# First loads of an attention + MoE kernel: k halves on two hardware queues, q halves by GpSimd, one staging buffer for the global queries and keys

## The chip, the cores and the metric

The kernel runs on one core of one Trainium2 chip. The core has five engines that run at their own pace and meet through semaphores: PE (TensorE, matrix products into the accumulator memory PSUM), DVE (VectorE), ACT (ScalarE), POOL (GpSimd) and SP (SyncE, which only issues transfers here). Transfers between the chip's memory and the core's SBUF run on 16 DMA engines that all issuers share; SP, ACT and POOL each have a queue of their own. Only POOL's transfers change the type on the way (f32 in memory to bf16 in SBUF).

The metric is the device time of one execution in microseconds (us). Beside it stands the profile of one execution: its span is the time between the first and the last instruction, a little less than the execution's own time.

## The reference

```
k_all = concat(k_g, k_l); v_all = concat(v_g, v_l)          # B=8, H=8, Sg=32, Sl=512, D=64
out_g = softmax(scale * q_g @ k_all.T) @ v_all              # 32 global queries see everything
s_ll  = where(|i-j| <= 32, scale * q_l @ k_l.T, -1e9)       # local queries see a band ...
s_lg  = scale * q_l @ k_g.T                                 # ... and the 32 global keys
out_l = softmax(concat(s_lg, s_ll)) @ concat(v_g, v_l)
x     = concat(out_g, out_l) as (8*544 tokens, 512)
h     = x @ w_in                                            # 512 -> 2048
out   = (h * sigmoid(1.702 h)) @ w_out                      # 2048 -> 512, f32
```

## The kernel before

Work is done batch by batch. A batch has two quads of four heads (`Quad(0)` and `Quad(1)` are the two of batch 0, named `a` and `c` in the code; `Wide` quads are all later ones). A quad's attention feeds `xL[b]`, the batch's hidden rows; `h_mm`/`h_step` multiply them by `w_in` and apply the activation (tanh form), `o_mm` multiplies by `w_out`. After the first batch, attention of the next batch is woven between these products, and PE is busy nearly without a break. The order on every engine is the order in which the code is written (a manual schedule); each engine runs its own instructions strictly in that order.

The change lies in the first 10 us, in how batch 0's first quad is fed. A quad needs its queries and keys as bf16 with the head dimension on the partitions. Data come in row layout into `rk` (keys) and `rq` (queries), and DVE transposes them: `Tk` into `kT`, `Tq` into `qt`, here in two halves each, (0,8) and (8,16). The 32 global queries and keys of the quad go the same way: `load_g32` brings them in f32, `cast_g32` (DVE) writes bf16 into `rqg`/`rkg`, `transpose_g` (DVE) gives `qgT`/`kgT`. `ext` then copies global queries from `qgT` into free rows beside the local queries (`qt`), for four windows c = 0 to 3 of keys, so that one product serves both.

How the first quad's inputs come in, in the kernel before:

- ACT's queue issues both k halves in f32 (line 144); ACT casts them to `rk` (line 651).
- SP's queue issues the global queries (line 132), then q's second half in f32 (line 146; ACT casts it, line 658), then the global keys (line 132).
- POOL's queue issues q's first half, cast on the way (line 145), then the mask's step function (line 153), then quad 1's k and q (line 81), the global values, v, constants, and the weights `w_in` (line 256; the first product `h_mm` waits for the third of these eight transfers).

Then the order on PE is: seven warm-up products (line 179), the additive band masks of quad 0 (`a.B`, line 337), filler products on zeros (`zero`, line 648), scores `a.S(0)` in two parts, `a.S(1)` and right behind it, in the same function, the global-by-global scores `gk` (line 373, global keys x global queries; they need `kgT`), more fillers, `c.B(0)`, `a.K()` (global keys x all local queries), `c.S(0)`, and so on up to `h_mm` (line 588). ACT runs the exponentials `X(0)` (line 387) and `X(1)` (line 382, four pieces; piece 2 holds the `gk` scores), then `XK`.

`qt` has 24 rows of 32; its first and last four are cleared by eight DVE memsets (lines 184, 185). `S` reads of these rows only the columns that `ext` writes.

Of the kernel before, what the change touches and what calls it, by code (L numbers as in the profile page):

```python
# [12 lines left out]
F32 = mybir.dt.float32  # L13
BF16 = mybir.dt.bfloat16
FP8 = mybir.dt.float8e4
AF = mybir.ActivationFunctionType
# [4 lines left out]
def kernel(  # L21
# [12 lines left out]
    nc = tc.nc  # L34

    B, H, Sl, D = q_l.shape
# [20 lines left out]
    consts = ctx.enter_context(tc.tile_pool(name="consts", bufs=1))  # L57
# [8 lines left out]
    qf = q_l.rearrange("b (u j) (r t) d -> b (j r) u (t d)", j=4, t=16)  # L66
    kf = k_l.rearrange("b (u j) (r t) d -> b (j r) u (t d)", j=4, t=16)
    qgf = q_g.rearrange("b (u j) s d -> (j s) (b u) d", j=4)
    kgf = k_g.rearrange("b (u j) s d -> (j s) (b u) d", j=4)
# [4 lines left out]
    def load(b, us=(0, 1), names="qk"):  # L74
        if b not in loaded:
            loaded[b] = (ld.tile([128, 2, 16 * D], BF16, name="rk"),
                         ld.tile([128, 2, 16 * D], BF16, name="rq"))
        s = slice(us[0], us[-1] + 1)
        for name in names:
            dst, src = ((loaded[b][0], kf), (loaded[b][1], qf))[name == "q"]  # L80
            nc.gpsimd.dma_start(out=dst[:, s], in_=src[b][:, s])  # L81
# [34 lines left out]
    def load_turned(eng, out_, in_):  # L116
        eng.dma_start(out=out_[32:128], in_=in_[0:96])  # L117
        eng.dma_start(out=out_[0:32], in_=in_[96:128])  # L118
# [5 lines left out]

    g32 = {}

    def load_g32(name, src):
        t = g32[name] = consts.tile([128, 2, D], F32, name="g32%s" % name)
        if name == "v":
            load_turned(nc.sync, t, src[:, 0:2, :])  # L130
        else:
            nc.sync.dma_start(out=t, in_=src[:, 0:2, :])

    def cast_g32(name, t):
        nc.vector.tensor_copy(t[:, 0:2, :D], g32[name])

    load(0, names="")
    rk, rq = loaded[0]
    early = ld.tile([128, 4, TB], F32, name="early", bufs=1)
    k32 = early[:, 0:2].rearrange("p a b -> p (a b)")  # L140
    halves = (slice(0, 8 * D), slice(8 * D, 16 * D))
    load_g32("q", qgf)
    for f in halves:
        nc.scalar.dma_start(out=k32[:, f], in_=kf[0][:, 0, f])
    nc.gpsimd.dma_start(out=rq[:, 0, halves[0]], in_=qf[0][:, 0, halves[0]])  # L145
    nc.sync.dma_start(out=early[:, 2], in_=qf[0][:, 0, halves[1]])
    load_g32("k", kgf)

    warm = consts.tile([128, 512], BF16)
    nc.vector.memset(warm, 0.0)  # L150
# [3 lines left out]
        out=step, in_=step, pattern=[[1, 289]], compare_op=ALU.is_ge,  # L154
# [26 lines left out]
    qtiles = []  # L181
    for i in range(4):
        qt = consts.tile([128, 24, 32], F32, name="q%d" % i)
        nc.vector.memset(qt[:, 0:4, :], 0.0)
        nc.vector.memset(qt[:, 20:24, :], 0.0)
        qtiles.append(qt)

    qgT = consts.tile([128, NQ, 40], F32)
# [44 lines left out]
    def transpose_g(lo, hi, names="qk"):  # L233
        for name, dst, s in (("q", qgT, rqg), ("k", kgT, rkg)):
            if name not in names:
                continue
            nc.vector.transpose(dst[:, lo:hi, :32], s[:, lo:hi].bitcast(F32))
# [406 lines left out]
    a, c = Quad(0), Quad(1)  # L644
# [2 lines left out]
        for _ in range(n):  # L647
            nc.tensor.matmul(ps[:m, :w], lhsT=warm[:, :m], rhs=warm[:, :w], start=False, stop=False, skip_group_check=True)

    def cast_k(f):  # L650
        nc.scalar.activation(rk[:, 0, f], k32[:, f], AF.Copy)

    cast_k(halves[0])
    cast_k(halves[1])
    cast_g32("q", rqg)
    transpose_g(0, 2, "q")
    a.ext((0, 1), True)
    nc.scalar.activation(rq[:, 0, halves[1]], early[:, 2], AF.Copy)
    a.Tk(0, 8)
    a.Tk(8, 16)  # L660
    a.Tq(0, 8)
    a.Tq(8, 16)
    a.ext((2, 3))
    cast_g32("k", rkg)
    transpose_g(0, 2, "k")
    load_rest()
# [9 lines left out]
    zero(16, a.bk[1][3], 32, 32)  # L676
    a.X(1)
    c.Tk()
    c.ext((0, 1))
    c.Tq()  # L680
    c.ext((2, 3))
    c.B(0)
    a.K()
    a.XK()
# [59 lines left out]
    a, c = nq[1]  # L744
# [41 lines left out]
    a, c = nq[2]  # L786
# [122 lines left out]
```

## Time and profile before

| | us |
|---|---|
| time, median of 3 executions | 299.23 (299.15 to 299.37) |
| the profiled execution's own time | 299.14 |
| its span | 297.4 |
| PE busy | 289.9 (97%) |
| DVE / ACT / POOL busy | 218.7 / 165.5 / 81.9 |
| DMA engines | 90% or more busy from 7.4 to 44.6 us, 70% in the first 7.4 us |

How to read it: the span is cut by the program's order into a front, some 18 us in which batch 0's attention is built up and PE is often waiting or running fillers, and the rest, in which PE goes from product to product. A row of the timeline gives the start, the busy time, the engine and line, the operation with its output and inputs, how many instructions were merged into the row, and in square brackets how long the engine had been idle and what ended that. A row of the transfers gives the median time from the start of the issuing instruction to the landing of the data. The share of DMA is the summed time of packets on 16 engines, and can exceed 1 since packets overlap on an engine.

### The profile page before, as it was taken

What the parts mean: (1) busy time and instruction counts of PE and PEld (TensorE: products, weight loads), DVE (VectorE), ACT (ScalarE), POOL (GpSimd) and SP (SyncE); (2) the same over time, 40 slices, a digit from 0 to 9 for tenths busy, and PEclk for the clock granted to TensorE, in tenths of its full rate; (3) what the DMA queues carried; (4) which work ended last, traced back from release to release, by engine and by line L of the source; (5) the groups of instructions that cost most, each with busy time, mean ns of one, the idle gap of its engine ahead of it and who ended that gap; (6) DMA issues with size and microseconds to landing.
All of it is one profiled execution on the core that took longest, in us unless ns stands there. A gap on an engine that the chain in (4) does not pass through costs nothing.

```text
span 297.4 us, 8162 instructions
## 1 busy us (share of the span) xinstructions
PE 289.9 (97%) x3403; PEld 149.8 (50%) x3444; DVE 218.7 (74%) x440; ACT 165.5 (56%) x252; POOL 81.9 (28%) x133
## 2 busy tenths in 40 slices
PE   8999999999999999999999999999999999999995
PEld 4544446445454455445454455445544455445653
DVE  6679888979867887778877887788878866683320
ACT  4827465585556745576447654666546651663421
POOL 8884630589565002700072003500000000000000
PEclk9999999999999999999999999999999999999999
DMA  7999994596999613961299115901130022101122
GB/s 177 178 206 211 204 160 86 119 138 100 192 212 160 124 37 68 150 122 29 47 96 178 29 41 87 109 0 39 36 72 2 2 48 63 35 2 35 35 66 78
DMA packets 59316, 28.06 MB, mean 94 GB/s; under 512 B 47376, under 2 KB 49808, under 8 KB 59280
## 3 DMA queue, kind: packets, MB, share of 16 engines
q0 software_dynamic: 51728, 17.70, 53.1%
q1 hardware_dynamic: 7264, 9.31, 12.3%
q8 instruction: 27, 0.44, 0.6%
q10 hardware_dynamic: 288, 0.52, 0.5%
q14 instruction: 9, 0.07, 0.1%
HBM read 36.31 MB, written 8.91 MB: 152 GB/s over the span
## 4 chain that ended last, share of the span: by engine, by line
PE 92%; POOL 3%; DMA 3%; issue 1%; ACT 0%; POOLq 0%
PE op L613 39%; PE hp L588 38%; PE s L533 6%; PE ov L559 5%; DMA w_in_sb<-in_moe_w_in_dram 3%; PE s L588 1%; PE op L625 1%; POOL v L243 1%; PE og L570 1%; POOL w_in_sb L256 0%; PE s L559 0%; POOL rq L145 0%; POOL rvg L117 0%; PE og L458 0%; POOL rvg L118 0%
## 5 line engine op out<-in xcount | busy, mean ns | idle before, releaser
L613 PE MATMUL op<-w_out_sb,gT 128*128 128x512 bf16 x497 | 119.4, 379 | 1.8 <-issue 0.3
L596 DVE SCALAR_TENSOR_TENSOR gT<-th,hp 128x512 bf16<-128x512 f32 (+1 forms) x140 | 91.0, 656 | 39.7 <-ACT th L595 38.7
L588 PE MATMUL hp<-xL,w_in_sb 128*128 128x512 bf16 x488 | 108.4, 379 | 0.4
L595 ACT ACTIVATE th<-hp 128x512 f32<-128x512 f32 (+1 forms) x140 | 79.8, 573 | 43.0 <-PE hp L588 41.1
L588 PEld LDWEIGHTS <-w_in_sb 128*128 128x128 bf16 x576 | 56.1, 98 | 64.2 <-issue 0.5
L613 PEld LDWEIGHTS <-gT 128*128 128x128 bf16 x528 | 49.3, 98 | 54.9
L544 ACT ACTIVATE e<-s 128x1016 bf16<-128x1016 f32 (+1 forms) x56 | 53.3, 1005 | 7.4 <-PE s L533 7.1
L628 ACT ACTIVATE ob<-op 128x512 f32<-128x512 f32 x32 | 18.9, 599 | 62.3 <-PE op L613 62.3
L97 POOL DMA_DIRECT2D v<-in_v_l_dram x35 | 28.1, 806 | 82.1 <-PE og L570 74.0
L549 DVE TENSOR_TENSOR e<-e,mask 128x1712 bf16<-128x1712 bf16 (+1 forms) x27 | 28.4, 1051 | 3.4 <-ACT e L544 3.4
L464 DVE STREAM_TRANSPOSE sT<-ov 128x512 f32<-128x512 f32 x15 | 10.7, 716 | 14.4 <-PE ov L559 12.6
L473 DVE TENSOR_TENSOR xL<-ov,rs 128x512 bf16<-128x512 f32 x30 | 19.4, 686 | 1.9 <-PE ov L440 0.5
L533 PE MATMUL s<-q,kT 32*128 32x160 bf16 (+3 forms) x672 | 19.2, 243 | 0.0
L533 PEld LDWEIGHTS <-kT 32*128 32x128 bf16 x672 | 13.1, 94 | 12.0 <-issue 6.9
L507 DVE STREAM_TRANSPOSE kT<-rk 128x512 f32<-128x512 f32 x14 | 14.5, 1035 | 0.7 <-DMA rk<-in_k_l_dram 0.7
L99 POOL DMA_DIRECT2D v<-in_v_g_dram x24 | 14.1, 586 | 0.6 <-issue 0.5
L468 DVE STREAM_TRANSPOSE rs<-rT 128x512 f32<-128x512 f32 x16 | 11.4, 711 | 0.6
L559 PE MATMUL ov<-e,v 128*32 128x128 bf16 (+3 forms) x624 | 11.7, 223 | 0.0
L312 DVE STREAM_TRANSPOSE q<-rq 128x512 f32<-128x512 f32 (+1 forms) x17 | 11.4, 672 | 0.1
L559 PEld LDWEIGHTS <-v 128*32 128x32 bf16 x672 | 10.5, 97 | 0.0
L588 PE MATMUL hp<-xG,w_in_sb 128*128 128x256 bf16 x64 | 9.6, 273 | 0.1
L81 POOL DMA_DIRECT2D rk<-in_k_l_dram x10 | 6.4, 639 | 2.6 <-DMA w_out_sb<-in_moe_w_out_dram 2.0
(103 smaller groups left out, 158.8 us busy)
## 6 DMA issues: line engine op xcount, KB each, us to landing
out_dram<-ob SPq DMA_DIRECT2D x128, 64.0 KB, 1.8
v<-in_v_l_dram POOLq DMA_DIRECT2D x28, 96.0 KB, 4.8
rq<-in_q_l_dram POOLq DMA_DIRECT2D x5, 512.0 KB, 6.5
rk<-in_k_l_dram POOLq DMA_DIRECT2D x5, 512.0 KB, 8.5
w_in_sb<-in_moe_w_in_dram POOLq DMA_DIRECT2D x8, 256.0 KB, 8.6
w_out_sb<-in_moe_w_out_dram POOLq DMA_DIRECT2D x4, 512.0 KB, 11.1
v<-in_v_l_dram POOLq DMA_DIRECT2D x11, 128.0 KB, 6.4
rk<-in_k_l_dram POOLq DMA_DIRECT2D x5, 256.0 KB, 9.1
```

The costliest lines, as they stand in the source:

```text
L97: nc.gpsimd.dma_start(out=vt[0:n, :, c, :D], in_=vs[FIRST[c] : FIRST[c] + n])
L473: nc.vector.tensor_mul(self.x[:, 2 * self.u + h, :], self.st[1 + h], self.st["rs"])
L507: nc.vector.transpose(flat[:, 0:Sl].rearrange("p (r t) -> p t r", t=16), loaded[self.b][0][:, self.u].bitcast(F32))
L533: nc.tensor.matmul(bank(self.ps, j)[:, at : at + n], lhsT=self.k[p, KEYS[c] : KEYS[c] + 128, e], rhs=self.q[p, lo:hi, r0 : r0 + nr, e], st ...
L544: nc.scalar.activation(self.E[rnd][:, 2 * i : 2 * i + 2, :n], self.ps[i][:, :, :n], AF.Exp, scale=scale)
L549: eng.tensor_mul(e, e, mask[:, rnd : rnd + 1, :n].to_broadcast([128, 4, n]))
L559: nc.tensor.matmul(ov[32 * j : 32 * j + 32, :].rearrange("p (t r) -> p t r", t=16)[:, t0:t1, r0 : r0 + nr], lhsT=lv, rhs=self.E[rnd][:, j, ...
L588: nc.tensor.matmul(hp[:, : width(i)], lhsT=w_in_c[:, fc // 8, kc, fc % 8 // 2, :, fc % 2], rhs=(xL[i] if i < B else xG)[:, kc, :], start=( ...
L595: nc.scalar.activation(th[:, :n], hp[:, :n], AF.Tanh, scale=0.851)
L596: nc.vector.scalar_tensor_tensor(gTs[i][:, fc, :n], in0=th[:, :n], scalar=1.0, in1=hp[:, :n], op0=ALU.add, op1=ALU.mult)
L613: nc.tensor.matmul(op, lhsT=gTs[i][:, fc, tci * 128 : tci * 128 + 128], rhs=w_out_sb[:, fc, :], start=(first and fc == 4 * f4), stop=(fc = ...
L628: nc.scalar.activation(ob, op, AF.Copy, scale=0.5)
```

## The change

- The two k halves are issued first, one on ACT's queue and one on SP's queue, instead of both on ACT's.
- The global queries follow k's second half on SP's queue. Before, they were first there.
- Both q halves come through POOL's casting transfers, one behind the other. q's second half no longer goes through SP in f32, and ACT's cast of it is gone.
- Global queries and keys share one f32 buffer `stage`. So the transfer of the global keys is issued by SP only when DVE's cast of the global queries has read the buffer. Before, they had buffers of their own and both transfers were issued at the start.
- DVE's order begins with `a.Tk(0, 8)`, then the cast and transpose of the global queries, then `a.Tk(8, 16)`, `a.Tq` twice, then the cast and transpose of the global keys, then `c.Tk` and `c.Tq`.
- All four `ext` copies of quad 0 and all four of quad 1 run on ACT, before `X(0)`. Before, two ran on ACT and six on DVE.
- The eight memsets of `qt` are gone.

```diff
+    stage = consts.tile([128, 2, D], F32, name="stage")
+
     def load_g32(name, src):
-        t = g32[name] = consts.tile([128, 2, D], F32, name="g32%s" % name)
-        if name == "v":
-            load_turned(nc.sync, t, src[:, 0:2, :])
-        else:
-            nc.sync.dma_start(out=t, in_=src[:, 0:2, :])
+        g32[name] = stage
+        nc.sync.dma_start(out=stage, in_=src[:, 0:2, :])
 ...
+    for f, eng in zip(halves, (nc.scalar, nc.sync)):
+        eng.dma_start(out=k32[:, f], in_=kf[0][:, 0, f])
     load_g32("q", qgf)
     for f in halves:
-        nc.scalar.dma_start(out=k32[:, f], in_=kf[0][:, 0, f])
-    nc.gpsimd.dma_start(out=rq[:, 0, halves[0]], in_=qf[0][:, 0, halves[0]])
-    nc.sync.dma_start(out=early[:, 2], in_=qf[0][:, 0, halves[1]])
-    load_g32("k", kgf)
+        nc.gpsimd.dma_start(out=rq[:, 0, f], in_=qf[0][:, 0, f])
 ...
-        nc.vector.memset(qt[:, 0:4, :], 0.0)
-        nc.vector.memset(qt[:, 20:24, :], 0.0)
 ...
-    cast_k(halves[0])
-    cast_k(halves[1])
+    for f in halves:
+        nc.scalar.activation(rk[:, 0, f], k32[:, f], AF.Copy)
+    a.Tk(0, 8)
     cast_g32("q", rqg)
+    load_g32("k", kgf)
     transpose_g(0, 2, "q")
-    a.ext((0, 1), True)
-    nc.scalar.activation(rq[:, 0, halves[1]], early[:, 2], AF.Copy)
-    a.Tk(0, 8)
+    a.ext(act=True)
+    c.ext(act=True)
     a.Tk(8, 16)
     a.Tq(0, 8)
     a.Tq(8, 16)
-    a.ext((2, 3))
     cast_g32("k", rkg)
     transpose_g(0, 2, "k")
 ...
     c.Tk()
-    c.ext((0, 1))
     c.Tq()
-    c.ext((2, 3))
     c.B(0)
```

More of the change, by code (lines that the diff above doesn't have):

```diff
@@ L138 @@
     rk, rq = loaded[0]
+    halves = (slice(0, 8 * D), slice(8 * D, 16 * D))
     early = ld.tile([128, 4, TB], F32, name="early", bufs=1)
     k32 = early[:, 0:2].rearrange("p a b -> p (a b)")
-    halves = (slice(0, 8 * D), slice(8 * D, 16 * D))
+    for f, eng in zip(halves, (nc.scalar, nc.sync)):
+        eng.dma_start(out=k32[:, f], in_=kf[0][:, 0, f])
     load_g32("q", qgf)
     for f in halves:
-        nc.scalar.dma_start(out=k32[:, f], in_=kf[0][:, 0, f])
-    nc.gpsimd.dma_start(out=rq[:, 0, halves[0]], in_=qf[0][:, 0, halves[0]])
-    nc.sync.dma_start(out=early[:, 2], in_=qf[0][:, 0, halves[1]])
-    load_g32("k", kgf)
+        nc.gpsimd.dma_start(out=rq[:, 0, f], in_=qf[0][:, 0, f])
     warm = consts.tile([128, 512], BF16)
@@ L648, in zero @@
             nc.tensor.matmul(ps[:m, :w], lhsT=warm[:, :m], rhs=warm[:, :w], start=False, stop=False, skip_group_check=True)
-    def cast_k(f):
+    for f in halves:
         nc.scalar.activation(rk[:, 0, f], k32[:, f], AF.Copy)
-    cast_k(halves[0])
-    cast_k(halves[1])
+    a.Tk(0, 8)
     cast_g32("q", rqg)
+    load_g32("k", kgf)
     transpose_g(0, 2, "q")
-    a.ext((0, 1), True)
-    nc.scalar.activation(rq[:, 0, halves[1]], early[:, 2], AF.Copy)
-    a.Tk(0, 8)
+    a.ext(act=True)
+    c.ext(act=True)
     a.Tk(8, 16)
```

## The prediction

> **What bounds the kernel now.** I read the chain of waits first, to see where a shift in the first 10 us would end.
>
> ```profile
> 10.59 7.73 DMA w_in_sb<-in_moe_w_in_dram
> 18.32 0.12 issue
> 18.44 1.67 PE s L588 x7
> ...
> 22.88 7.23 PE hp L588 x32
> ```
>
> From 18.44 us on the chain is PE alone to the end (PE has 92% of it; its POOL and DMA parts lie before 18.44). Nothing later absorbs a shift: what delays the first `h_mm` at 18.44 delays the end by as much. That start has two parents: the third `w_in` transfer, landing at 18.32, and PE's own earlier work, which ends at 17.79 + 0.49 = 18.28. So the front can gain at most 0.16 us from PE's side alone, while every microsecond that PE comes later counts, less 0.16.
>
> Next the timeline of PE, ACT and DVE, for what holds PE's side.
>
> ```profile
> 7.78 0.39 DVE L135 CAST rkg<-g32k 128x128 bf16<-128x128 f32 x1
> 8.03 0.92 PE L354 MATMUL s<-q,kT 32*128 32x80 bf16 x32
> 8.20 0.24 DVE L237 STREAM_TRANSPOSE kgT<-rkg 128x64 f32<-128x64 f32 x1
> 8.49 1.66 ACT L387 ACTIVATE e<-s 128x856 bf16<-128x856 f32 x2 [1.29 <-PE s L354]
> 8.88 0.22 PE L373 MATMUL s<-qgT,kgT 32*32 32x32 bf16 x8
> 9.26 1.09 PE L648 MATMUL s<-warm 128*128 128x512 bf16 x18 [0.16 <-issue]
> 10.28 0.78 PE L337 MATMUL s<-bias,ident 128*128 128x160 bf16 x8
> ```
>
> `kgT` is ready at 8.44, and PE comes to its first reader, `gk`, at 8.88: 0.44 us of slack. Behind `gk` stand the fillers, `c.B(0)` 1.40 us after it, `a.K`, `c.S(0)`, and with them `XK` (11.69) and `c.X(0)` (12.25) on ACT. PE runs in order, so all of it moves with `gk`.
>
> Third, the transfers: those of SP's and ACT's queues issued at 1.3 to 2.4 us, then SP's output stores in 75 to 90 us and in 105 to 120 us, and the share of DMA at such times.
>
> ```profile
> early<-in_k_l_dram ACTq DMA_DIRECT2D x1, 256.0 KB, 4.4
> early<-in_q_l_dram SPq DMA_DIRECT2D x1, 256.0 KB, 4.8
> ...
> g32k<-in_k_g_dram SPq DMA_DIRECT2D x1, 64.0 KB, 5.9
> ```
>
> ```profile
> out_dram<-ob SPq DMA_DIRECT2D x12, 64.0 KB, 5.2
> ```
>
> ```profile
> out_dram<-ob SPq DMA_DIRECT2D x12, 64.0 KB, 1.7
> ```
>
> ```profile
> 6.00:7.00 1.00, 1.00 (x14) 0.74 (x12) 0.60 (x2) 1.00 (x4) 1.00 (x2) 1.00 1.11 198
> ...
> 80.00:85.00 5.00, 4.89 (x130) 2.98 (x130) 3.13 (x5) 2.52 (x3) 3.49 (x5) 1.00 1.47 209
> ```
>
> The same 64 KB on SP's queue take 1.7 us where the DMA engines are idle and 5.2 us (groups of 4.7 to 6.7) where POOL's loads fill them; the last two figures of a window are that share and GB/s. From 3 us on the share is 0.94 or more, so a transfer issued at 6 us meets the loaded case.
>
> **The change, part by part.**
>
> *k halves.* Half 1 is issued at 0.82 instead of 1.28. Before, half 0 landed at 3.81 and half 1 at 5.74, where ACT's casts started. Two equal halves now share the engines; 512 KB at the 335 GB/s of 3 to 4 us is 0.76 us more than 256 KB for half 0 at worst. I take 4.3 for both (3.8 to 4.6). ACT casts half 0 by 4.95 and `Tk(0,8)` runs on DVE from 5.0 (cast to transpose was 0.70: 3.81 to 4.51). In the Trainium skill, "DMA: Bandwidth & Descriptors", section "Issuing engines are not separate DMA queues", says that several issuers save only the time to start a transfer. By that, half 1 would gain the 0.46 us of issue and land at 5.3, with `Tk(8,16)` still ahead of 6.40; the sum below would be the same.
>
> *Global queries.* Now issued at 1.29, behind 256 KB on SP's queue. At best 3.1 us as the lone first transfer took (0.82 to 3.94): 4.4. At worst the 4.8 of q's half, second on that queue: 6.1. I take 5.6, nearer the second, which has the same place. DVE is free for the cast only behind `Tk(0,8)`, at 5.0 to 5.5. So the cast starts at 5.65 (5.0 to 6.1) instead of 3.99 and takes 0.32.
>
> *Global keys, the added wait.* SP issues them once this cast has ended, at 6.0 (5.4 to 6.5) instead of 1.84. On SP nothing is queued behind: its next instruction is the first output store at 45.76. On DVE the cast of the keys waits, and behind it the transpose, `c.Tk` and `c.Tq`; on PE all behind `gk`. Issue to landing: not below 3.1 (the global queries in an empty machine), not above 6.7 (the slowest loaded store). The nearest rows are 4.8 (a load of this queue, half loaded), 5.2 (64 KB, loaded) and 5.9 (this very load, behind 256 KB); I take 5.0. They land at 11.0 instead of about 7.7. Cast to `kgT` was 7.78 to 8.44, 0.66, and I add 0.06 for PE to see it: `gk` at 11.7 (9.2 to 13.9) instead of 8.88, that is 2.8 later (0.3 to 5.0).
>
> Does PE's side give any of it back? `XK` waits for `a.K` and `c.X(0)` for `c.S(0)`, both on PE behind `gk`. `c.Tk` (1.01) and `c.Tq` (0.71) end by 13.4, ahead of `c.S(0)` at 11.55 + 2.8 = 14.4. ACT's pieces of `X(1)` wait with the fillers. Nothing: the score chain moves whole.
>
> *q halves by POOL.* One more issue of 0.70 stands ahead of the step function (2.10) and all later POOL work. `ident` and `bias` on DVE move from 2.70 and 3.08 to about 3.4 and 3.8, still ahead of the first mask product at 4.23, which the warm-up products hold up anyway. Half 1, issued at 2.0, lands by POOL's 5.4 to 5.7 us at 7.4 to 7.7; its transpose ran at about 7.27. So scores may come 0 to 0.5 later, all under the wait for `gk`; without that cover, up to 0.5 lost. `w_in` is issued at 9.9 instead of 9.18; its landing follows the bytes ahead of it, unchanged as read from memory, so 18.3 to 19.0: hidden, with PE's side at 21 us; without that cover, up to 0.7.
>
> *`ext` on ACT.* Two took 0.41, so eight take 1.64, less the two and the cast of q (0.61) that ran there before: 0.62 more. From `qgT` at 6.25 they end at 7.9, before `X(0)` at 8.49, in the 1.29 us that ACT sat idle. DVE loses 1.1 us of copies, and all memsets (8 of 0.17, before 2.6 us, under the wait for the global queries). Both are worth nothing here. `Tk(8,16)` starts at 5.65 + 0.52 = 6.2 instead of 6.40, worth nothing while `gk` waits.
>
> **The sum.** 2.84 later at `gk`, less the 0.16 that `h_mm` waited for `w_in`: +2.7 us. The profiled execution took 299.14 (span 297.4 and 1.7 around it; 0.09 below the median, inside the spread shown). Forecast 301.8, with the ends of the terms 299.3 to 304.0.
>
> **The rivals.**
>
> *The global keys come in time.* If their load met idle engines, 1.7 to 3.1 us from 5.4 to 6.0, `kgT` would be there at 7.9 to 9.9, and `gk` at 8.88 or a little later. This is the one case that ends on the other side: it decides from a landing before 8.2. Then the k halves lead: `Tk(8,16)` is up to 0.2 earlier, `w_in` bounds at 18.3, and the time is 299.0 (298.5 if `w_in` also comes 0.5 earlier; 299.6 if it comes 0.5 later). The share of 1.11 in 6 to 7 us and the 5.9 us of this same load speak against it. The same page's section "Anatomy of one DMA — SWDGE (gpsimd) path" fits 2.0 us plus bytes over 436 GB/s, for a transfer of GpSimd; as an estimate, 2.15 us here, so 299.0 by it. This trace disagrees for a loaded machine: 5.2 us.
>
> *Late, and PE falls back to a slow clock.* The seven warm-up products start 0.42 us apart, the 32 of `hp` at 22.88 in 7.23 us, 0.23 each: in its first microseconds PE runs at half pace, though the granted clock reads 1.00. Idle for 9.0 to 11.7, it might fall back. Fillers (3 x 0.2), `c.B(0)` (8 x 0.07), `a.K` (0.4) and `c.S(0)` (0.4) at half pace add 2.0 us: 303.8. For it: the long gap. Against: PE was busy right before. "TensorE: Matmul & The Clock Gate" in the Trainium skill (Part 1) puts the return to the slow clock at an idle window of about 3.4 us, longer than the gap forecast; no gap of that length is in this trace.
>
> **How the numbers follow.** Late global keys 0.76, around 301.8; late with the slow clock 0.12, at 303.8; in time 0.12, at 299.0. The range 299.9 to 304.0 takes in the first to both ends but for its most favourable tenth, and part of the second. A difference within 0.2% (0.6 us) can't be told from none: of the in-time case 0.04 is faster and 0.08 the same; the rest, 0.88, is slower.
>
> **What would show it.** Right: the transfer of the global keys issued near 6 us and landing near 11; DVE idle before the cast of `rkg` for 2 us or more; PE idle before the `gk` products for 2 us or more; `h_mm` near 21 without a wait for `w_in`. Step by step: k's second cast well ahead of 5.74, the global queries' cast at 5.0 to 6.1, no wait of `X(0)` for `ext`. Wrong: the keys landing within 3 us of issue, or `gk` waiting for scores or q's second half instead.

## The result

The changed kernel takes 302.51 us (median of 4, 301.97 to 303.58) against 299.19 before (median of 4): a ratio of 1.0116, interval 1.0087 to 1.0145. It is slower, inside the range and 0.7 us above the forecast of 301.8.

The chain of waits of the changed kernel passes through the load that the change made wait, then through PE. Columns: start, length, what.

```profile
5.66 5.02 DMA stage<-in_k_g_dram
10.68 0.02 issue
10.70 0.46 DVE rkg L134
11.16 0.02 issue
11.18 0.26 DVE kgT L233
11.44 0.04 issue
11.48 0.24 PE s L369 x7
...
22.91 1.67 PE s L584 x7
```

`gk` (now line 369) starts at 11.48 instead of 8.88, 2.60 later, and `h_mm` (now line 584) at 22.91 instead of 18.44, 4.47 later. The two profiled executions differ by 303.58 - 299.14 = 4.44, so nothing is given back behind `h_mm`. But the wait explains only 2.60 of it. The other 1.87 come between `gk` and `h_mm`: 9.56 us before, 11.43 after. The same stretch in the timeline of the changed kernel:

```profile
4.30 1.15 ACT L647 ACTIVATE rk<-early 128x512 bf16<-128x512 f32 x2 [1.78 <-DMA early<-in_k_l_dram]
...
5.44 0.20 DVE L134 CAST rqg<-stage 128x128 bf16<-128x128 f32 x1
...
5.66 0.37 SPq L131 DMA_DIRECT2D stage<-in_k_g_dram  x1
...
7.52 0.92 PE L350 MATMUL s<-q,kT 32*128 32x80 bf16 x32
...
7.97 1.66 ACT L383 ACTIVATE e<-s 128x856 bf16<-128x856 f32 x2 [0.67 <-PE s L350]
...
10.70 0.45 DVE L134 CAST rkg<-stage 128x128 bf16<-128x128 f32 x1 [3.32 <-DMA stage<-in_k_g_dram]
...
11.48 0.24 PE L369 MATMUL s<-qgT,kgT 32*32 32x32 bf16 x8 [3.04 <-DVE kgT L233]
...
12.05 1.60 PE L644 MATMUL s<-warm 128*128 128x512 bf16 x18 [0.33 <-issue]
...
13.58 1.35 PE L333 MATMUL s<-bias,ident 128*128 128x160 bf16 x8
```

The fillers took 1.09 before and take 1.60, the eight mask products 0.78 and 1.35. The windows of the changed kernel say why; the third figure from the end is the granted clock of TensorE.

```profile
8.00:9.00 1.00, 0.44 (x16) 0.12 (x8) 0.00 (x0) 1.00 (x2) 0.94 (x4) 1.00 1.47 181
9.00:10.00 1.00, 0.00 (x0) 0.00 (x0) 0.00 (x0) 1.00 (x3) 0.87 (x8) 0.81 2.35 159
10.00:11.00 1.00, 0.00 (x0) 0.00 (x0) 0.30 (x1) 0.47 (x2) 1.00 (x2) 0.50 2.44 155
...
15.00:16.00 1.00, 1.00 (x16) 0.15 (x12) 0.00 (x0) 0.04 (x1) 1.00 (x2) 0.50 1.17 193
16.00:17.00 1.00, 1.00 (x36) 0.45 (x28) 0.00 (x0) 0.84 (x2) 1.00 (x2) 0.77 1.25 206
17.00:18.00 1.00, 1.00 (x32) 0.55 (x20) 0.24 (x1) 1.00 (x2) 0.54 (x2) 1.00 1.23 203
```

PE went idle at 8.44. In finer windows the clock falls to half at 9.63 and returns at 16.45, 6.8 us later. Such a stretch at half clock is called a spell below. The mean clock of this execution is 0.989; the other three, which were not profiled, have 0.994. As an estimate that is one spell of about half that length (0.006 x 301 / 0.5 = 3.6 us). They take 301.97, 302.45 and 302.58.

### The profile page after: what moved, and what is told of

The parts are those of the page before. It is cut to its first block, busy times and chain, and to the rows that moved or that the text cites. A ratio compares the mean times of both kernels' runs of the same rounds, so it can differ in the third digit from the quotient of the medians.

```text
span 301.9 us, 8153 instructions
## 1 busy us (share of the span) xinstructions
PE 291.3 (97%) x3403; PEld 150.2 (50%) x3444; DVE 216.7 (72%) x426; ACT 166.4 (55%) x257; POOL 82.7 (27%) x134
## 4 chain that ended last, share of the span: by engine, by line
PE 93%; DMA 3%; issue 1%; ACT 1%; DVE 1%
PE op L609 38%; PE hp L584 38%; PE s L529 6%; PE ov L555 5%; DMA stage<-in_k_g_dram 2%; PE s L584 1%; PE op L621 1%; DMA early<-in_k_l_dram 1%; PE og L566 1%; PE s L333 1%; ACT e L383 1%; PE s L644 1%; PE s L350 0%; PE ov L436 0%; PE s L555 0%
## 5 line engine op out<-in xcount | busy, mean ns | idle before, releaser
L555 PE MATMUL ov<-e,v 128*32 128x128 bf16 (+3 forms) x624 | 11.7, 223 | 0.0
```

Of the source, the lines that this page charges most:

```text
L555: nc.tensor.matmul(ov[32 * j : 32 * j + 32, :].rearrange("p (t r) -> p t r", t=16)[:, t0:t1, r0 : r0 + nr], lhsT=lv, rhs=self.E[rnd][:, j, ...
```

## The experiments

Each is compared with runs of the kernel before on the same chip. In some executions of the kernel before the mean clock was 0.992 to 0.994 as well, and the time 300.7 to 302.0 (14 of 90), so two medians are given where they differ: of all runs, and of those with a clock of 0.998 or more ("full clock").

**e1_own_buffers: the change without the shared buffer**

```diff
-    stage = consts.tile([128, 2, D], F32, name="stage")
     def load_g32(name, src):
-        g32[name] = stage
-        nc.sync.dma_start(out=stage, in_=src[:, 0:2, :])
+        t = g32[name] = consts.tile([128, 2, D], F32, name="g32%s" % name)
+        nc.sync.dma_start(out=t, in_=src[:, 0:2, :])
```

> The changed kernel with one f32 buffer each for the global queries and keys, so that SP issues the keys' load at 1.8 us, right behind the queries'. Theory (the loss is the wait for the shared buffer and what follows from it): the keys land by about 7.5, gk finds kgT ready, scores start 0.5 us earlier than in the kernel before (6.8 against 7.3), PE keeps its clock, and h_mm starts when the third w_in transfer lands, 18.3 to 18.6: 298.9 to 299.5. Rival (POOL's extra casting load, or the eight copies on ACT, cost by themselves): 300.5 or more, with gk or X(0) waiting for something else.

Measured: 298.81 (11 runs) against 299.25; ratio 0.9984 (0.9975 to 0.9993). The timeline of this run:

```profile
6.86 0.26 DVE L132 CAST rkg<-g32k 128x128 bf16<-128x128 f32 x1
...
7.49 0.92 PE L348 MATMUL s<-q,kT 32*128 32x80 bf16 x32
...
8.33 0.22 PE L367 MATMUL s<-qgT,kgT 32*32 32x32 bf16 x8
...
17.66 2.07 PE L582 MATMUL s<-xL,w_in_sb 128*128 128x512 bf16 x8
```

The whole loss is gone, and a gain of 0.44 us is left. So the q halves by POOL and the copies on ACT cost nothing here; the shared buffer is the cause of the loss. PE comes to `h_mm` 0.55 us earlier than before, as it came to `gk` (8.33 against 8.88). The start to compare with is 18.21, that of the first weight load for `h_mm` in the kernel before: eight weight loads are recorded there and only seven products, from 18.44 on, so the record of the first product is missing. In this run the eight products take 2.07 instead of the 1.90 of the same eight without a wait, and the start of `a.Gm` behind them is 19.67 instead of 20.05: 0.17 of the 0.55 are lost inside them, to the third `w_in` transfer.

**e2_shared_only: the kernel before with the shared buffer alone**

```diff
-    load_g32("k", kgf)
 ...
     cast_g32("q", rqg)
+    load_g32("k", kgf)
```

(with one `stage` tile as in the change)

> The kernel before with only the shared buffer: the keys' load is issued behind the cast of the queries. Theory: that cast starts at 4.0 as before, SP issues at about 4.4, the load takes 4.5 to 5.0 us in the loaded machine and lands near 9.2, gk comes at about 9.9 instead of 8.88: 1.0 later, less 0.16, so 300.0 (299.7 to 300.4), with no loss of clock since PE waits only 1 us. Rival (the wait costs only together with the new order of the other loads): 299.2.

Measured: 300.69 in the one run at full clock, 302.63, 301.85 and 301.94 in three with a clock of 0.994. From the chain and the timeline of the first:

```profile
4.36 5.49 DMA stage<-in_k_g_dram
...
10.43 0.22 PE s L371 x8
```

```profile
10.43 0.22 PE L371 MATMUL s<-qgT,kgT 32*32 32x32 bf16 x8 [1.44 <-DVE kgT L235]
```

The wait alone does it, without the other parts of the change: +1.4 us at full clock. Between the two profiled executions it is 300.69 - 299.14 = 1.55, exactly what `gk` moved (10.43 - 8.88). The load took 5.49, above the 4.5 to 5.0 expected, and the time lies above the expected range. The profiled execution kept its clock through an idle of 1.44 us, as expected; the three others lost it, against the expectation, at 1.2 to 1.9 us more. They were not profiled, so their gaps are not known.

**e3_fillers and e9_fewer_fillers: zero products in the gap ahead of gk**

```diff
             if split:
+                zero(12, ps[3])     # e9_fewer_fillers: zero(8, ps[3])
                 self.gk(ps[2][:, RW : RW + 32], self.qg)
```

> The changed kernel with 12 more filler products of 512 columns between the scores of a.S(1) and gk, 2.6 us of PE work in the gap of 3.0. Theory (part of the loss is PE's half clock after the gap): gk still at 11.5, but PE keeps its full clock, and the front ends 2.6 later than before less 0.16: 301.6 (301.3 to 301.9), and runs differ less from each other. Rival (the clock is no part of it, the wait is all): no change from the changed kernel, 302.5.

> The changed kernel with 8 fillers ahead of gk instead of 12: 1.7 us of work, ended before the keys are there. Theory (a gap of 3 us drops the clock, a shorter rest of it does not): gk starts when kgT is ready, 10.3 to 11.5 by the keys' load of 4.1 to 5.0 us, at full clock: 300.5 to 301.6, below the 301.3 with 12. Rival (any rest of the gap drops the clock): 302 or more.

Measured: with 12, 301.32 (301.09 to 301.72, 5 runs, all at full clock). With 8, 301.55 of all 12 runs, 301.40 of the eleven at full clock, and 303.62 in one with 0.994. From the timeline with 8:

```profile
7.60 0.92 PE L350 MATMUL s<-q,kT 32*128 32x80 bf16 x32
8.68 1.67 PE L645 MATMUL s<-warm 128*128 128x512 bf16 x7 [0.16 <-issue]
11.49 0.22 PE L370 MATMUL s<-qgT,kgT 32*32 32x32 bf16 x8 [1.14 <-DVE kgT L233]
...
21.05 1.67 PE L585 MATMUL s<-xL,w_in_sb 128*128 128x512 bf16 x7 [0.16 <-DVE rT L463]
```

With 8 fillers `gk` starts at 11.49, as in the changed kernel without them (11.48), so this pair separates the two parts of the loss. From `gk` to `h_mm` it is 21.05 - 11.49 = 9.56, as in the kernel before, and not the 11.43 of the changed kernel: with the clock kept, the 1.87 are gone. At full clock the wait costs 301.40 - 299.25 = 2.15 us in the median, and 301.7 - 299.14 = 2.56 in the two profiled executions. Measured from the 301.40, the clock adds 0.6 to 1.2 in the three executions of the changed kernel with a clock of 0.994 (301.97 to 302.58) and 2.2 in the one with 0.989 (303.58). More work on PE made the kernel faster by 1.0 us (302.51 to 301.55). The 12 fillers were themselves the bound in their profiled run (`gk` at 11.29, `kgT` there at 10.3, since the load took 4.1). That fits 8 and 12 coming out alike, against the expectation that 8 would be faster.

**e4_keys_alone: the keys' load in an idle machine**

```diff
-    load(0, (1,), "kq")
-    load_turned(nc.gpsimd, rvg[:, 0:2, :D], vgf[:, 0:2])
 ...
     transpose_g(0, 2, "k")
+    late = consts.tile([128, 8], BF16, name="late")
+    nc.gpsimd.tensor_copy(late, rkg[:, 0, 0:8])
+    load(0, (1,), "kq")
+    load_turned(nc.gpsimd, rvg[:, 0:2, :D], vgf[:, 0:2])
     load_rest()
```

> The changed kernel with all of POOL's loads behind the two q halves held back until DVE has cast the global keys (a small POOL copy reads the cast). The whole gets slower, since weights come later; only the keys' load is looked at. Theory (its 5.0 us are the machine's load, POOL's transfers on the same 16 engines): issued at 5.7, lands within 3.3 us, gk by 9.7. Rival (5.0 us are this load's own cost, with its 256-byte rows): again 4.5 us or more.

Measured: the load, issued at 5.54 us, takes 2.0 us (it took 5.0 in the changed kernel, from 5.66); `gk` starts at 8.14, right behind the scores. First this run's transfers, then its windows, where the last two figures are the share of DMA and GB/s, then the transfers and a window of the changed kernel:

```profile
stage<-in_k_g_dram SPq DMA_DIRECT2D x1, 64.0 KB, 2.0
```

```profile
6.00:7.00 1.00, 0.46 (x20) 0.31 (x19) 0.85 (x3) 1.00 (x8) 0.00 (x0) 1.00 0.26 60
7.00:8.00 1.00, 1.00 (x46) 0.84 (x42) 0.41 (x2) 0.43 (x3) 0.15 (x2) 1.00 0.02 5
```

```profile
stage<-in_k_g_dram SPq DMA_DIRECT2D x1, 64.0 KB, 5.0
```

```profile
6.00:7.00 1.00, 1.00 (x26) 0.81 (x28) 0.82 (x3) 1.00 (x7) 1.00 (x3) 1.00 1.12 181
```

So 3.0 of the 5.0 us are the load that POOL's transfers put on the shared engines, not this load's short rows. The time of the run, 303.71 in its one execution, says nothing about this: its weights and quad 1's inputs come later.

**e10_k_split_only and e11_q_by_pool_only: the two new routes, each alone on the kernel before**

```diff
+    for f, eng in zip(halves, (nc.scalar, nc.sync)):          # e10_k_split_only
+        eng.dma_start(out=k32[:, f], in_=kf[0][:, 0, f])
     load_g32("q", qgf)
-    for f in halves:
-        nc.scalar.dma_start(out=k32[:, f], in_=kf[0][:, 0, f])
```

```diff
-    nc.gpsimd.dma_start(out=rq[:, 0, halves[0]], in_=qf[0][:, 0, halves[0]])      # e11_q_by_pool_only
-    nc.sync.dma_start(out=early[:, 2], in_=qf[0][:, 0, halves[1]])
+    for f in halves:
+        nc.gpsimd.dma_start(out=rq[:, 0, f], in_=qf[0][:, 0, f])
 ...
-    nc.scalar.activation(rq[:, 0, halves[1]], early[:, 2], AF.Copy)
```

> The kernel before with the k halves issued first, one on ACT's and one on SP's queue; all else as before (q's second half in f32 behind the global queries on SP, cast by ACT, own buffers). Theory (k's second half held the scores): both halves cast by 5.5, the first part of the scores 0.5 us earlier, but q's second half now stands behind k's on SP, lands at 6.5 or later and is cast by ACT, so the second part and X(0) gain 0 to 0.3: 299.0 (298.8 to 299.3). Rival (the split alone makes the whole gain of own buffers): 298.8.

> The kernel before with both q halves by POOL's casting loads (no f32 half on SP, no cast on ACT); the k halves stay both on ACT's queue, the global queries stay first on SP's. Theory: the scores still wait for k's second half, landed at 5.5 to 5.7, so nothing is gained, and POOL's queue is 0.6 later without effect: 299.2 (299.0 to 299.4). Rival (the lighter SP queue makes the gain): 298.8.

Measured against 299.20: the split alone 299.46 (ratio 1.0012, 0.9990 to 1.0033; 299.44 against 299.19 at full clock), q by POOL alone 298.74 (0.9982, 0.9971 to 0.9992). My theory had these the wrong way round. The timeline of ACT, first with the split alone, then with q by POOL alone:

```profile
4.18 1.15 ACT L651 ACTIVATE rk<-early 128x512 bf16<-128x512 f32 x2 [1.66 <-DMA early<-in_k_l_dram]
...
7.21 0.63 ACT L658 ACTIVATE rq<-early 128x512 bf16<-128x512 f32 x1 [1.56 <-DMA early<-in_q_l_dram]
8.82 1.66 ACT L387 ACTIVATE e<-s 128x856 bf16<-128x856 f32 x2 [0.98 <-PE s L354]
```

```profile
3.94 0.63 ACT L651 ACTIVATE rk<-early 128x512 bf16<-128x512 f32 x1 [0.90 <-DMA early<-in_k_l_dram]
4.78 0.63 ACT L651 ACTIVATE rk<-early 128x512 bf16<-128x512 f32 x1 [0.21 <-DMA early<-in_k_l_dram]
...
8.18 1.66 ACT L387 ACTIVATE e<-s 128x856 bf16<-128x856 f32 x2 [2.46 <-PE s L354]
```

Once q's second half no longer goes over SP's queue in f32, k's second half, still second on ACT's queue, is there by 4.78 instead of 5.74. The split brings it by 4.8 too, but q's second half then stands behind it, and its cast at 7.21 holds the scores: `X(0)` at 8.82 instead of 8.49. So the gain of the change, less its shared buffer, comes from the route of q. Which part of it, the earlier k or the missing cast on ACT, was not separated. The gain is one of the medians: the profiled execution of q by POOL alone is the slowest of its twelve (299.31), because in it `h_mm`, 0.31 us early with its first product (17.90), waits until 18.56 for `w_in` with the second.

**e5_own_buffers_order, e6_before_order, e12_q_by_pool_order: the wait for the third w_in transfer**

```diff
-    for fc in range(4):
-        h_mm(0, fc, bank(pt, fc), (0, 1))
+    for kc in (0, 1):
+        for fc in range(4):
+            h_mm(0, fc, bank(pt, fc), (kc,))
     a.Gm()
```

> The kernel with own buffers, and the first eight h_mm products of the batch ordered by rows of w_in (first the four of the first 128 rows, then the four of the next) instead of by output group. The second product of the old order waits for the third w_in transfer, the four of the first rows need only the first transfer. Theory (with own buffers PE is ready at 17.7 and loses 0.4 us inside these eight products to that transfer): the 0.4 are gained, 298.4 against 298.8. Rival (PE bounds here by itself): 298.8.

> The kernel before with the same order of the first eight h_mm products alone. Theory: PE is ready at 18.28 and the third transfer lands at 18.32, so 0.1 to 0.2 us are gained, not to be told from none: 299.1. Rival (the order itself, not the earlier readiness, makes the gain of the other run): 298.8.

> The kernel before with both q halves by POOL, and the first eight h_mm products ordered by rows of w_in. Theory (with q by POOL alone PE is ready at 17.9, starts its first product, and waits 0.4 us for the third w_in transfer; four products fit in that time): 298.3 to 298.5 instead of 298.7. Rival (the runs whose w_in is late are those whose PE is late, too, and the order gives nothing, as it did with own buffers): 298.7.

Measured: 298.77 with own buffers (0.9956, 0.9932 to 0.9980, against all runs of the kernel before, 9 of 35 of which had the lower clock; 299.25 for those at full clock), 299.34 on the kernel before (no difference), 298.81 with q by POOL (0.9976, 0.9959 to 0.9993). Without the order it was 298.81, 299.34 and 298.74. The order gains nothing that can be told. With own buffers the profile had only 0.17 us to gain, not the 0.4 expected. In the profiled execution of e12_q_by_pool_order the wait is gone (`h_mm` from 17.91 without a break, `a.Gm` at 19.74, against 20.18 in e11_q_by_pool_only), but the medians do not follow. If the wait of 0.4 us is rare in the other executions of e11_q_by_pool_only, whose profiled one is its slowest, that would explain it; it is not shown.

**e8_ext_on_dve: own buffers, and the copies back on DVE**

```diff
-    a.ext(act=True)
-    c.ext(act=True)
+    a.ext((0, 1), True)
 ...
     a.Tq(8, 16)
+    a.ext((2, 3))
 ...
     c.Tk()
+    c.ext((0, 1))
     c.Tq()
+    c.ext((2, 3))
```

> The kernel with own buffers, and the ext copies where they were before (two on ACT, six on DVE). Theory (the copies lie in idle time on either engine): as with own buffers, 298.8 (298.7 to 298.9). Rival (the move to ACT is worth something, or costs something): 0.2 us or more to one side.

Measured: 298.95 (12 runs, 298.57 to 299.85) against 299.25 at full clock, beside 298.81 and 298.77 with the copies on ACT. No difference clear of the spread.

## Why the prediction was right, and where not

*The added wait.* Right in place and size. The cast of the queries began at 5.44 (forecast 5.65), SP issued at 5.66 (6.0), the load took 5.0 (5.0), `gk` came at 11.48 (11.7). e1_own_buffers shows that taking this wait away takes all of the loss, e2_shared_only that it makes one by itself. The choice of the loaded rows over the idle ones decided the forecast: e4_keys_alone measured 2.0 us in an idle machine, and `gk` did not wait there. The fit of the Trainium skill for transfers of GpSimd ("DMA: Bandwidth & Descriptors", section "Anatomy of one DMA — SWDGE (gpsimd) path") gives 2.15 us for 64 KB as an estimate, close to the 2.0 of this load on SP's queue. That 5.0 was met to the digit is luck: the same load took 4.1 in e3_fillers and 5.5 in e2_shared_only.

*The 0.16 taken off.* This term of the sum is wrong. I read the idle of 0.16 before 18.44 as a wait for `w_in`, but the first of the eight `h_mm` products is missing from the record of the kernel before; its weights were loaded at 18.21, and `a.Gm` behind the eight starts at 20.05, 1.84 later. From the first product to `a.Gm` it is 1.83 in e2_shared_only and 1.84 in e3_fillers, where all eight are recorded and none waits. So PE alone held this start, and a shift of `gk` passes on whole: 1.55 of 1.55 in e2_shared_only. Nor is 0.16 the most that an earlier front can gain: e1_own_buffers gained 0.44. It is also the second of these products and not the first that can wait for the third `w_in` transfer, as e11_q_by_pool_only shows (17.90 and 18.56).

*Nothing gives it back.* Right: `h_mm` and the end moved together, 4.47 and 4.44.

*The slow clock.* This is the step that failed. The main case put the cost of the clock at nothing. It was a rival with 0.12, at 303.8, and it happened in all four runs (302.45 and 302.58 at the middle, 303.58 in the profiled one). Its price of 2.0 us was nearly met by the profiled run: 1.87, of which the fillers, `c.B(0)`, `a.K` and `c.S(0)` have 0.70, 0.58, 0.41 and 0.18, against the forecast 0.6, 0.56, 0.4 and 0.4. What misled was the argument against it: that PE had been busy right before, and that the gap is shorter than the idle window of about 3.4 us that the Trainium skill gives in "TensorE: Matmul & The Clock Gate" (Part 1). Here the clock fell 1.2 us after PE went idle, so for the fall the measurement decides against that reading. The lengths of the spells agree with the window of 3413 ns that the same page of the Trainium skill states: 3.41 us in e4_keys_alone and 6.83, two of them, in the changed kernel. At full clock (e9_fewer_fillers, 301.40) the main case would have been met within 0.4 us. That 302.51 still lies inside the range is owed to the width left for the load's latency and to the part of the rival in it: some 1.1 us of it, 302.51 less 301.40, are the clock.

*k halves.* Landing right (casts from 4.30 on, forecast 4.3), and e10_k_split_only shows that the earlier issue does it with q's half still on SP's queue. But that is not the only way, and it was not enough: e11_q_by_pool_only has k's second half as early (4.78) while it stays second on ACT's queue, and in e10_k_split_only the scores came later all the same, held by q. The rule of the Trainium skill that several issuers save only the time to start a transfer ("DMA: Bandwidth & Descriptors", section "Issuing engines are not separate DMA queues") would give 0.46 us, by the prediction's estimate. k's second half gained 0.96 (5.74 to 4.78) without any earlier issue of its own, so what else was in flight counted for more than the issue.

*q halves by POOL.* The second half landed by 6.93 (forecast 7.4 to 7.7), and both parts of the scores were 0.5 us early (6.82 against 7.33, 7.52 against 8.03), all lost under `gk`. Costed at 0 to 0.5 of a loss, the route is worth 0.46 of a gain (298.74 against 299.20) where `gk` does not wait.

*`ext` on ACT and the memsets.* Right that the copies are worth nothing: ACT still sat idle 0.67 before `X(0)`, waiting for PE, and e8_ext_on_dve is not different. They have little room, though: in the profile of e5_own_buffers_order, where the global queries were cast late (5.73), the first scores waited last for ACT's copies, at 7.32. The memsets were not tried by themselves.

## What to carry to other kernels

When two loads are put into one buffer, the second load's whole latency goes onto the path of whoever needs it, and that latency must be read from transfers that ran while the DMA engines were loaded, not from the first ones in an empty machine: here 5.0 us against 2.0. A gap on PE can cost more than its length, since PE can come out of it at half clock; here a few products on zeros in the gap bought 1 us back. Of the two routes that the change redrew, only moving q's f32 half off SP's queue paid; with buffers of their own for the global queries and keys it gives 298.7 to 298.8, faster than both kernels. And count the records before reading a short wait: eight weight loads beside seven products meant that the wait in front of them was none.

## What the runs showed of the hardware

The granted clock of TensorE fell to half 1.2 us after PE went idle in the changed kernel (a gap of 3.0 us) and 3.9 us after in e4_keys_alone (a gap of 4.2 us). It was kept through idle stretches of 1.44 us in the profiled execution of e2_shared_only, 1.37 in that of e6_before_order and 1.14 in that of e9_fewer_fillers. The spells seen last 6.83 and 3.41 us.

By their mean clock, three of the four executions of e2_shared_only lost it, and so did 14 of 90 of the kernel before. With e6_before_order and e10_k_split_only, which also bring q's second half over SP's queue, it is 19 of 114; the five versions with own buffers and both q halves by POOL (e1, e5, e8, e11, e12) lost it in none of 59. The profile of the kernel before shows gaps of 0.2 us at most in the front, but that of e6_before_order, with the same front, one of 1.37; the executions of the kernel before that lost the clock were not profiled, so their gaps are not known. What PE activity keeps the clock was not measured.

The same 64 KB load on SP's queue, issued between 4.4 and 5.7 us, took 2.0 us with a DMA share of 0.3 or less, and 4.1 to 5.5 us with POOL's loads beside it (a share of 0.8 to 2.4).
